# Factors of two levels made behind chosen products, and one sum moved behind a product, in a lightning attention and tanh-shrink kernel

## The chip, the cores and the metric

The kernel runs on one core of a Trainium2 chip. The metric is the device time in microseconds (us) of one execution; lower is better. Before the change it is 693.81 us, the median of three runs (693.71 to 694.52).

## The reference

A causal linear attention with decay runs in blocks, and its output goes through a feed-forward block that keeps `h - tanh(h)`. All is fp32.

```python
# q, k, v: (4, 8, 768, 64); lam: one decay for each of 8 heads
for b in range(nb):                     # blocks of 64 positions, state carried along
    intra = einsum('bhic,bhjc->bhij', qb, kb) * Dmask   # lam ** (i - j) where i >= j
    intra = einsum('bhij,bhjd->bhid', intra, vb)
    inter = einsum('bhid,bhde->bhie', qb * lam_pow, kv_state)
    out[:, :, sl] = intra + inter
    kv_state = lam_block * kv_state + einsum('bhsd,bhse->bhde', kb * rev_pow, vb)
x = out as (4 * 768 tokens, 512)
h = x @ w_in                            # w_in: 512 x 2048
return (h - tanh(h)) @ w_out            # w_out: 2048 x 512
```

## The kernel before, in words

The sequence is cut into six groups of 128 positions; a group is 128 positions of all four batches, 512 tokens. For each group the attention makes its block of x, the "up" product makes h and the activation, and the "down" product makes the output. Group 0 multiplies plainly (`up_plain`, L579, and `down_plain`, L595). While it does, the factors of later groups are made from the weights and stored in a DRAM tensor `factors`. In groups 1 to 5 the two large products use a scheme of seven products for a 2 x 2 split (Winograd's form of Strassen's): for each of them, sums of the four quarters on VectorE (DVE), and seven multiplications on TensorE (PE) instead of eight.

**Up.** The hidden size is cut into four units u. In each unit the products are numbered 1, 2, 6, 5, 7, 4, 3; `up(g, u, n)` makes product n with 8 matmuls records (L393) into one of the PSUM banks y (ya or yb, alternating by unit), z or w. ScalarE (ACT) copies out y (L406, L411, L413) and makes the tanh (L401); DVE adds the banks (L408, L414, L419), takes off the tanh (L402) and makes sums (L422, L423). L414 reads z behind product 5, and product 3 then adds into the same z. Product 1 of the next unit is written ahead of products 4 and 3.

**Down.** The down product also has seven products P1 to P7. P1, P2 and P6 are plain (`down`, L496) and each read four pieces of a factor. P4, P5, P7 and P3 are split once more into seven by the same scheme (`down_twice`, L539), so each needs seven factors of a second level, `fine`. These are made once, in the second group (g = 1), from four quarters of a factor: `load_quarters(n)` brings them from `factors` (L444, issued by GpSimd (POOL)), `factors_twice(n)` makes four sums on DVE (L459) and writes seven tiles to the DRAM tensor `fine` (L461). This happens for four products, TWICE = (4, 5, 7, 3); below they are sets 0 to 3. In the program before, set u is loaded at the start of unit u and made behind product 7 of unit u. P1 is written behind product 7 of the last unit, ahead of that unit's products 4 and 3.

The quarters share a ring of seven SBUF tiles with the pieces of the down products: `piece` (L470 from `fine`, L473 from `factors`) issues loads up to seven ahead of use, on POOL's queue.

**Sums of the hidden block.** Behind P2, `down` makes S2 into tile g11 and then S4 into tile g21 (L508), one instruction per unit for each. Inside `down_twice`, sums s1 and s2 are made by `sums_twice` (L522 to L524), and L544 takes s2 off a quarter once the second of the seven parts was multiplied; the sixth part multiplies that quarter.

**Attention of the next group.** Its pieces are written in between: `run(p0...)` and `run(p1...)`. From group 2 on, q and k come as blocks of 32 x 32 in tiles q_blk and k_blk (L136, 16 DMAs for a tile, issued by SyncE (SP)), in a ring of seven tiles, and DVE transposes them (L271) to qt and kt and scales qt (L281). Loads of all four batches of a group are issued by SP one tile after the other.

The order of each engine's queue is set by the tile framework's scheduler: it takes the program's order as priority and places instructions by its own model of time, so an instruction can stand in its engine's queue ahead of one that is written before it.

Of the kernel before, what the change touches and what calls it, by code (L numbers as in the profile page):

```python
# [14 lines left out]
AL = mybir.AluOpType  # L15
# [8 lines left out]
def kernel(  # L24
# [31 lines left out]
    nc = tc.nc  # L56
# [8 lines left out]
    NU = DFF // 512  # L65
# [312 lines left out]
    def hidden(g, c):  # L378

        if (g, c) not in hid:  # L380
            hid[g, c] = gpool.tile([128, NU, 2, HB], F32, name=f"g{c}", tag=f"g{c}")
        return hid[g, c]

    def up(g, u, n):
        a, bname = FACT[n]
        wt = {"A11": w1[u][:, 0:2, 0], "A12": w1[u][:, 2:4, 0], "S3": w1[u][:, 0:2, 1], "A22": w1[u][:, 2:4, 1],
              "S1": ws[u][:, 0], "S2": ws[u][:, 1], "S4": ws[u][:, 2]}[a]
        x = xt[g][bname] if bname != "B11" else xt[g, 0][:, 0:2]
        key = ("up", g, u)
        t, first = product_bank(key, n)  # L390
        for m in range(2):
            for kt in range(2):
                nc.tensor.matmul(out=t[:, m, :], lhsT=wt[:, kt, ts(m, 128)], rhs=x[:, kt, :],  # L393
                                 start=first and m == 0 and kt == 0, stop=kt == 1, skip_group_check=True)

        def dst(c):
            return hidden(g, c)[:, u]

        def finish(c, src):
            th = work.tile([128, 2, HB], F32, name="th", tag="th")  # L400
            nc.scalar.activation(th, src, AF.Tanh)  # L401
            nc.vector.tensor_tensor(dst(c), src, th, op=AL.subtract)  # L402

        y, z, w = (banks[key, x].rearrange("q (m c) -> q m c", m=2) if (key, x) in banks else None for x in "yzw")
        if n == 1:
            nc.scalar.activation(dst(11), y, AF.Copy)  # L406
        elif n == 2:
            nc.vector.tensor_tensor(dst(11), dst(11), w, op=AL.add)  # L408
            finish(11, dst(11))
        elif n == 6:  # L410
            nc.scalar.activation(dst(12), y, AF.Copy)  # L411
        elif n == 7:
            nc.scalar.activation(dst(22), y, AF.Copy)  # L413
            nc.vector.tensor_tensor(dst(22), dst(22), z, op=AL.add)  # L414
            finish(22, dst(22))
        elif n == 4:
            finish(21, y)
        elif n == 3:
            nc.vector.tensor_tensor(dst(12), dst(12), z, op=AL.add)  # L419
            finish(12, dst(12))  # L420

            nc.vector.tensor_tensor(dst("S1"), dst(12), dst(22), op=AL.add)  # L422
            nc.vector.tensor_tensor(dst(12), dst(11), dst(12), op=AL.subtract)  # L423
# [4 lines left out]
    TWICE = (4, 5, 7, 3)  # L428
# [19 lines left out]
    def load_quarters(n):  # L448
        for i in range(2):
            for j in range(2):  # L450
                quarters[n, i, j] = late["pool"].tile([128, NU, 128], F32, name="wq", tag="wb", bufs=RING)
                factor_block(quarters[n, i, j], XAT[FACT[n][1]], i, j)

    def factors_twice(n):

        b11, b12, b21, b22 = (quarters.pop((n, i, j)) for i in range(2) for j in range(2))
        t1, t2, t4 = (late["pool"].tile([128, NU, 128], F32, name=f"wt{x}", tag="sums", bufs=4) for x in (1, 2, 4))
        for dst, x, y in ((t1, b12, b11), (t2, b22, t1), (b12, b22, b12), (t4, b21, t2)):
            tc.keep_in_program_order(nc.vector.tensor_tensor(dst, x, y, op=AL.subtract))  # L459
        for i, t in enumerate((b11, b21, t2, t1, b12, b22, t4)):  # L460
            nc.gpsimd.dma_start(out=fine[TWICE.index(n), i], in_=t)  # L461
# [23 lines left out]

    res, low = {}, {}

    def down(g, n):

        t, first = product_bank(("down", g), n)  # L490
        a = hidden(g, HIDAT[FACT[n][0]])
        for u in range(NU):
            wb = piece(g, n, u)
            for m in range(2):
                for kt in range(2):
                    nc.tensor.matmul(out=t[:, m, :], lhsT=a[:, u, kt, ts(m, 128)], rhs=wb[:, kt, :],  # L496
                                     start=first and u == 0 and m == 0 and kt == 0, stop=u == NU - 1 and kt == 1,
                                     skip_group_check=True)
        t = t.rearrange("q m c -> q (m c)")
        if n == 1:  # L500
            res[g, 11] = late["pool"].tile([128, 512], F32, name="o11", tag="o11", bufs=1)
            nc.scalar.activation(res[g, 11], t, AF.Copy)
        elif n == 2:
            nc.vector.tensor_tensor(res[g, 11], res[g, 11], t, op=AL.add)
            store(g, 11, res[g, 11])
            for x, y, z in ((11, "S1", 11), (21, 21, 11)):
                for u in range(NU):
                    nc.vector.tensor_tensor(hidden(g, x)[:, u], hidden(g, y)[:, u], hidden(g, z)[:, u], op=AL.subtract)  # L508
        else:
            res[g, "U2"] = otile("u2")  # L510
            nc.scalar.activation(res[g, "U2"], t, AF.Copy)
            nc.vector.tensor_tensor(res[g, 4], res[g, 4], res[g, "U2"], op=AL.add)
# [14 lines left out]
    def down_twice(g, n, zw):  # L527
        a11, a12, a21, a22 = quarter(g, n)
        s1, s2 = low.pop((g, n))
        y = bank("y2", "yb", 1)[:, 0:128]  # L530
        zw = bank("zw", zw, 1)
        o = res[g, n] = otile(f"q{n}")
        r5 = late["pool"].tile([128, 128], F32, name="r5", tag="r5", bufs=2)
        for x, a, dst, keep in ((1, a11, y, o[:, 0:128]), (2, a12, zw[:, 0:128], None), (6, s2, y, o[:, 128:256]),
                                (5, s1, zw[:, 128:256], r5), (7, a21, y, o[:, 384:512]), (3, a12, zw[:, 128:256], None),
                                (4, a22, y, o[:, 256:384])):
            wb = piece(g, n, x).rearrange("p m c -> p (m c)")
            for u in range(NU):
                nc.tensor.matmul(out=dst, lhsT=a[:, u, :], rhs=wb[:, ts(u, 128)], start=x in (1, 2) and u == 0,  # L539
                                 stop=u == NU - 1, skip_group_check=True)  # L540
            if keep is not None:
                nc.scalar.activation(keep, dst, AF.Copy)  # L542
            if x == 2:
                nc.vector.tensor_tensor(a12, a12, s2, op=AL.subtract)  # L544
        nc.vector.tensor_tensor(o[:, 384:512], o[:, 384:512], r5, op=AL.add)
        nc.vector.tensor_tensor(o[:, 0:256], o[:, 0:256], zw[:, 0:256], op=AL.add)
        if n == 5:

            nc.vector.tensor_tensor(res[g, 5], res[g, 5], res[g, "U2"], op=AL.add)
        elif n == 7:  # L550
            nc.vector.tensor_tensor(res[g, 4], res[g, 4], o, op=AL.add)
            store(g, 21, res[g, 4])
            nc.vector.tensor_tensor(o, o, res[g, 5], op=AL.add)
            store(g, 22, o)
        elif n == 3:
            nc.vector.tensor_tensor(o, o, res[g, 5], op=AL.add)
            store(g, 12, o)
# [45 lines left out]
    def run(pieces):  # L603
        for fn, *args in pieces:
            fn(*args)
# [30 lines left out]
            sums_in(kt - KH + NU)  # L636
    early.close()
    late["pool"] = ctx.enter_context(tc.tile_pool(name="late", bufs=1))
    up(1, 0, 1)
    for g in range(1, NG):  # L640
        last = g == NG - 1
        p0, p1 = attention(g + 1) if not last else ([], [])
        for u in range(NU):
            if g == 1:
                load_quarters(TWICE[u])
            for n in (2, 6, 5, 7):
                up(g, u, n)
            if g == 1:
                factors_twice(TWICE[u])
            if u + 1 < NU:  # L650
                up(g, u + 1, 1)
            else:
                down(g, 1)
            up(g, u, 4)
            up(g, u, 3)
            if not last and u > 1:
                run(p0[u - 2:u - 1])
        sums_twice(g, 4)
        down(g, 2)
        run(p0[2:])  # L660
        sums_twice(g, 5)
        down_twice(g, 4, "z")
        run(p1[0:1])
        sums_twice(g, 7)
        down(g, 6)
        run(p1[1:2])
        down_twice(g, 5, "w")
        if not last:
            sums_twice(g, 3)
        run(p1[2:])  # L670
        down_twice(g, 7, "z")
        if not last:
            up(g + 1, 0, 1)
            down_twice(g, 3, "z")
        else:
            down_end(g)
# [30 lines left out]
```

## Time and profile before

| | |
|---|---|
| median of 3 runs | 693.81 us (693.71 to 694.52) |
| profiled execution: time, span | 692.45 us, 690.6 us |
| PE, PEld busy | 671.1, 576.1 us |
| DVE, ACT, POOL busy | 428.3, 191.0, 170.0 us |
| granted clock, mean | 0.995 |
| DMA | 116.43 MB, mean 169 GB/s |
| chain that ended last | PE 84%, issue 6%, DMA 5%, POOL 3% |

The span is the time from the first instruction to the last; the execution's own time has 1.85 us around it. PE is busy for 97% of the span, so the chain of work that ended last is nearly PE's own sequence. PEld is the weight load, which overlaps the matmuls. The slices of the page give the busy share along the span; the second group's up products run from 154 to 200 us, and its down products follow.

### The profile page before, as it was taken

The page shows a single profiled execution, that of the slowest core. Times are in us where ns is not written, and L with a number is a line of the kernel's source. Part 1 is how long each engine was busy: PE and PEld are TensorE (multiplying, and loading weights), DVE is VectorE, ACT ScalarE, POOL GpSimd, SP SyncE. Part 2 cuts the span into 40 slices and gives each one's busy share as a digit, 9 for nine tenths or more (in the row PEclk, how much of TensorE's full clock was granted, in tenths as well). Part 3 has the DMA queues.
Part 4 walks back from the last instruction along what each step waited for, and adds up shares of the span by engine and source line. Part 5 has one row for each costly group of instructions (what it writes and reads, how often), then busy time and mean ns, then how long its engine had stood idle before and what let it go on. Part 6 is the DMA issues. An engine that isn't in the chain of part 4 may idle for free.

```text
span 690.6 us, 12075 instructions
## 1 busy us (share of the span) xinstructions
PE 671.1 (97%) x4568; PEld 576.1 (83%) x4568; DVE 428.3 (62%) x747; ACT 191.0 (28%) x372; POOL 170.0 (25%) x302
## 2 busy tenths in 40 slices
PE   6999999999969999999999999999999999999998
PEld 5788855558758899888899888899988899988897
DVE  3897766995566864347865447766356756354732
ACT  2764433323221112332112332112233112233110
POOL 0001212124643335001244100134200234300252
PEclk9999999999998999999999999999999999999999
DMA  9869959468996688355498902588800366500374
GB/s 189 225 212 235 280 166 257 151 151 251 270 266 201 184 248 237 87 102 111 121 252 238 214 11 46 139 224 229 234 1 10 114 189 199 178 1 1 115 248 155
DMA packets 158393, 116.43 MB, mean 169 GB/s; under 512 B 133120, under 2 KB 133504, under 8 KB 158336
## 3 DMA queue, kind: packets, MB, share of 16 engines
q0 software_dynamic: 25472, 84.95, 37.9%
q1 hardware_dynamic: 132720, 30.71, 23.0%
q8 instruction: 36, 0.59, 0.4%
q14 instruction: 21, 0.17, 0.1%
q10 hardware_dynamic: 144, 0.00, 0.0%
HBM read 94.64 MB, written 20.97 MB: 167 GB/s over the span
## 4 chain that ended last, share of the span: by engine, by line
PE 84%; issue 6%; DMA 5%; POOL 3%; DVE 1%; ACT 1%; POOLq 0%
PE y L393 16%; PE y L496 10%; PE y L539 10%; PE z L393 8%; PE h L579 8%; PE zw L539 7%; PE w L496 5%; PE op L595 4%; PE w L393 4%; PE sp L291 3%; DMA wq<-factors 3%; PE op L342 3%; POOL fine L461 1%; PE kv L311 1%; PE op L336 1%
## 5 line engine op out<-in xcount | busy, mean ns | idle before, releaser
L470 POOL DMA_DIRECT2D wb<-fine x133 | 71.5, 538 | 135.6 <-PE w L496 44.3
L473 POOL DMA_DIRECT2D wb<-factors x64 | 34.7, 544 | 208.5 <-PE y L496 180.3
L496 PE MATMUL y<-wb,g 128*128 128x256 f32 x320 | 73.4, 390 | 6.3 <-issue 6.3
L496 PEld LDWEIGHTS y<-wb,g 128*128 128x128 f32 x320 | 62.3, 196 | 15.3 <-issue 6.7
L393 PE MATMUL y<-xt,w 128*128 128x256 f32 x320 | 73.2, 380 | 0.0
L393 PEld LDWEIGHTS y<-xt,w 128*128 128x128 f32 x320 | 60.5, 190 | 8.5 <-issue 0.5
L401 ACT ACTIVATE th<-g 128x512 f32<-128x512 f32 x60 | 37.7, 630 | 91.6 <-DVE g L419 43.4
L402 DVE TENSOR_TENSOR g<-g,th 128x512 f32<-128x512 f32 x60 | 41.4, 690 | 27.4 <-ACT th L401 27.1
L595 PE MATMUL op<-wt,g 128*128 128x512 f32 x128 | 56.5, 596 | 0.0
L579 PE MATMUL h<-xt,w 128*128 128x256 f32 x256 | 56.1, 381 | 0.0
L579 PEld LDWEIGHTS h<-xt,w 128*128 128x128 f32 x256 | 48.4, 190 | 7.2 <-issue 0.3
L542 ACT ACTIVATE q<-y 128x128 f32<-128x128 f32 x76 | 21.1, 277 | 99.3 <-PE y L539 99.3
L595 PEld LDWEIGHTS op<-wt,g 128*128 128x128 f32 x128 | 23.9, 190 | 27.7 <-issue 27.0
L539 PE MATMUL y<-wb,g 128*128 128x128 f32 x336 | 45.3, 278 | 0.0
L414 DVE TENSOR_TENSOR g<-g,z 128x512 f32<-128x512 f32 x20 | 13.7, 686 | 48.0 <-ACT g L413 48.0
L539 PEld LDWEIGHTS y<-wb,g 128*128 128x128 f32 x336 | 41.2, 192 | 1.1 <-issue 0.3
L393 PE MATMUL z<-tt,ws 128*128 128x256 f32 x160 | 37.9, 380 | 1.1 <-DVE g L419 1.1
L393 PE MATMUL w<-xt,w 128*128 128x256 f32 x160 | 37.8, 379 | 0.0
L393 PE MATMUL y<-tt,w 128*128 128x256 f32 x160 | 37.8, 379 | 0.0
L393 PE MATMUL y<-tt,ws 128*128 128x256 f32 x160 | 37.8, 379 | 0.0
L393 PE MATMUL z<-xt,ws 128*128 128x256 f32 x160 | 37.8, 379 | 0.0
L496 PE MATMUL w<-wb,g 128*128 128x256 f32 x160 | 35.8, 382 | 0.0
(120 smaller groups left out, 1153.3 us busy)
## 6 DMA issues: line engine op xcount, KB each, us to landing
wb<-fine POOLq DMA_DIRECT2D x133, 256.0 KB, 3.6
wb<-factors POOLq DMA_DIRECT2D x64, 256.0 KB, 5.3
raw<-in_moe_w_out_dram POOLq DMA_DIRECT2D x16, 512.0 KB, 4.7
v_nat<-in_v_dram SPq DMA_DIRECT2D x24, 256.0 KB, 5.1
factors<-wt POOLq DMA_DIRECT2D x8, 768.0 KB, 5.3
k_nat<-in_k_dram SPq DMA_DIRECT2D x20, 256.0 KB, 5.1
raw<-in_moe_w_in_dram SPq DMA_DIRECT2D x8, 512.0 KB, 5.0
raw<-in_moe_w_in_dram SPq DMA_DIRECT2D x16, 256.0 KB, 5.6
```

Source lines behind the costliest of these rows:

```text
L291: nc.tensor.matmul(out=sp[j][:, p, :], lhsT=kt[ts(j, 64), p, :], rhs=qt[ts(j, 64), p, :], start=True, stop=True)
L342: nc.tensor.matmul(out=dst(n, p, j), lhsT=vn[:, 2 * p + j, :], rhs=ss[:, j, p, :], start=g == 0 and n == 0 and p % 2 == 0, stop=n == 1 and ...
L393: nc.tensor.matmul(out=t[:, m, :], lhsT=wt[:, kt, ts(m, 128)], rhs=x[:, kt, :], start=first and m == 0 and kt == 0, stop=kt == 1, skip_gro ...
L401: nc.scalar.activation(th, src, AF.Tanh)
L402: nc.vector.tensor_tensor(dst(c), src, th, op=AL.subtract)
L470: nc.gpsimd.dma_start(out=t.rearrange("p m c -> p (m c)"), in_=fine[TWICE.index(n_), SUB.index(x_)].rearrange("p u c -> p (u c)"))
L473: nc.gpsimd.dma_start(out=t, in_=factors[XAT[FACT[n_][1]]][:, 2 * x_:2 * x_ + 2, :])
L496: nc.tensor.matmul(out=t[:, m, :], lhsT=a[:, u, kt, ts(m, 128)], rhs=wb[:, kt, :], start=first and u == 0 and m == 0 and kt == 0, stop=u = ...
L539: nc.tensor.matmul(out=dst, lhsT=a[:, u, :], rhs=wb[:, ts(u, 128)], start=x in (1, 2) and u == 0, stop=u == NU - 1, skip_group_check=True)
L542: nc.scalar.activation(keep, dst, AF.Copy)
L579: nc.tensor.matmul(out=hm[:, m, :], lhsT=w1[u][:, i, a, ts(m, 128)], rhs=xt[0, t][:, i, :], start=m == 0 and i == 0, stop=i == KI - 1, ski ...
L595: nc.tensor.matmul(out=obank[b], lhsT=g, rhs=wt[:, 2 * a:2 * a + 2, :], start=kt == 0 and a == 0, stop=kt == KH - 1 and a == 1)
```

## The change

The quarters of set 0 are loaded ahead of the second group. In that group a counter runs over the products in the order of writing (seven for each unit: 2, 6, 5, 7, then product 1 of the next unit, or P1 behind the last unit, then 4, 3). Behind the 4th, 10th, 15th and 20th of them the sums of set 0, 1, 2 and 3 are written, and at once the loads of the set after it. The 10th is product 5 of unit 1, the 15th is product 2 of unit 2 and the 20th is product 4 of unit 2. So set 3 is written ahead of P1, and not inside unit 3. This only concerns g = 1; the products' own order is the same in all groups.

S4 (into g21) is written behind P4 (`down_twice(g, 4, "z")`) and no longer behind P2; this concerns all five groups. P3, which reads it, comes later still.

```diff
+    def sums_once(g, dst, x, y):
+
+        for u in range(NU):
+            nc.vector.tensor_tensor(hidden(g, dst)[:, u], hidden(g, x)[:, u], hidden(g, y)[:, u], op=AL.subtract)
+
     def down(g, n):
...
             store(g, 11, res[g, 11])
-            for x, y, z in ((11, "S1", 11), (21, 21, 11)):
-                for u in range(NU):
-                    nc.vector.tensor_tensor(hidden(g, x)[:, u], hidden(g, y)[:, u], hidden(g, z)[:, u], op=AL.subtract)
+            sums_once(g, 11, "S1", 11)
...
+    turns, made = (4, 10, 15, 20), []
+    load_quarters(TWICE[0])
     up(1, 0, 1)
     for g in range(1, NG):
...
         for u in range(NU):
-            if g == 1:
-                load_quarters(TWICE[u])
-            for n in (2, 6, 5, 7):
-                up(g, u, n)
-            if g == 1:
-                factors_twice(TWICE[u])
-            if u + 1 < NU:
-                up(g, u + 1, 1)
-            else:
-                down(g, 1)
-            up(g, u, 4)
-            up(g, u, 3)
+            for n in (2, 6, 5, 7, 1, 4, 3):
+                if n != 1:
+                    up(g, u, n)
+                elif u + 1 < NU:
+                    up(g, u + 1, 1)
+                else:
+                    down(g, 1)
+                if g == 1:
+                    made.append(n)
+                    if len(made) in turns:
+                        t = turns.index(len(made))
+                        factors_twice(TWICE[t])
+                        if t + 1 < len(TWICE):
+                            load_quarters(TWICE[t + 1])
             if not last and u > 1:
                 run(p0[u - 2:u - 1])
         sums_twice(g, 4)
...
         down_twice(g, 4, "z")
+        sums_once(g, 21, 21, 11)
         run(p1[0:1])
```

The lines of the kernel after the change stand a few further down: L496 becomes L501, L508 becomes L491, L539 becomes L542 and L544 becomes L547; L459 and what is ahead of it stay.

## The prediction

> **What bounds the kernel now.** I read the page's busy shares first: TensorE (PE) is busy 671.1 of 690.6 us, so only its gaps can be won and any new gap is lost in full. The waits of PE say where the gaps are; the two that lie in the second group (the stretch from 154 to 240 us) are:
>
> ```profile
> PE y L496 <- issue: 6.3, 1, 6.3
> PE z L393 <- DVE g L419: 1.1, 1, 1.1
> ```
>
> The first is the start of product P1 (down, n = 1), at 206.84 us; the profile names no releaser. The windows view shows what the pause costs beyond itself. Its columns are the length, then the busy time of PE, PEld, DVE, ACT and POOL, the granted clock, the share of the DMA engines, and GB/s:
>
> ```profile
> 204.00:206.00 2.00, 0.00 (x0) 0.00 (x0) 1.55 (x3) 0.42 (x1) 0.55 (x1) 0.83 0.92 265
> 207.00:208.00 1.00, 1.00 (x3) 0.82 (x4) 0.00 (x0) 0.00 (x0) 0.00 (x0) 0.50 0.49 142
> 212.00:213.00 1.00, 1.00 (x6) 0.81 (x5) 0.52 (x1) 0.00 (x0) 0.00 (x0) 0.92 0.88 175
> ```
>
> The clock halves at 205.33 (0.83 over 2 us is two thirds at 1.00 and a third at 0.50) and is whole again at 212.16 (0.92 likewise). PE works at half rate from 206.84 to 212.16, 5.32 us, and loses 2.66. The chain shows P1 taking 9.78 us where later P1s take 6.91. So this place costs 6.30 + 2.87, and with the 1.1 us wait 10.3 us in all: the most that the change can win.
>
> The DVE timeline (start, duration, what, idle before and its releaser) shows the work that is moved, and the place that decides my forecast:
>
> ```profile
> 175.57 0.69 DVE L414 TENSOR_TENSOR g<-g,z 128x512 f32<-128x512 f32 x1 [2.42 <-ACT g L413]
> ...
> 181.51 0.69 DVE L459 TENSOR_TENSOR wt<-wq,wt 128x512 f32<-128x512 f32 x1 [3.26 <-DMA wq<-factors]
> 182.12 0.69 DVE L459 TENSOR_TENSOR wq<-wq 128x512 f32<-128x512 f32 x1
> ...
> 235.94 0.69 DVE L544 TENSOR_TENSOR g<-g,s 128x512 f32<-128x512 f32 x1 [1.28 <-PE zw L539]
> ...
> 239.89 0.71 DVE L271 STREAM_TRANSPOSE qt<-q_blk 128x512 f32<-128x512 f32 x1
> 240.52 0.67 DVE L271 STREAM_TRANSPOSE kt<-k_blk 128x512 f32<-128x512 f32 x1
> 241.12 0.65 DVE L281 TENSOR_TENSOR qd<-qt,fwd 128x512 f32<-128x512 f32 x1
> 241.69 0.70 DVE L271 STREAM_TRANSPOSE qt<-q_blk 128x512 f32<-128x512 f32 x1
> 245.55 0.71 DVE L271 STREAM_TRANSPOSE kt<-k_blk 128x512 f32<-128x512 f32 x1 [3.16 <-DMA q_blk<-in_q_dram]
> ```
>
> L544 subtracts s2 inside down_twice(1, 4), the TensorE product P4, and PE's sixth part of P4 needs its result:
>
> ```profile
> 238.42 1.06 PE L539 MATMUL zw<-wb,g 128*128 128x128 f32 x8
> ```
>
> The last transpose, kt of the fourth batch (b = 3), waits until 245.55 for its tile. The SP timeline says why it is so late:
>
> ```profile
> 210.44 9.85 SPq L136 DMA_DIRECT2D k_blk<-in_k_dram  x16
> 220.81 11.96 SPq L136 DMA_DIRECT2D q_blk<-in_q_dram  x16
> 232.88 7.54 SPq L136 DMA_DIRECT2D k_blk<-in_k_dram  x16
> ```
>
> The eight tiles of group 2 (16 issues each) leave SP one after the other from 156.53; k_blk of b = 3 is the eighth and leaves at 232.88 to 240.42.
>
> [...] L459 waits 3.26 us for its quarter and the next instruction, L402 at 183.32, waits behind it. [...] 16 SP issues take 7.5 us while the engines are 23% busy (287.82 on) and 11.96 at 79%.
>
> **The change, part by part.** Nothing is added or taken out; the compiled order has the same matmuls in the same order on PE. What moves:
>
> (a) *Factors on DVE.* There are four sets of four quarters; each takes four subtractions L459, about 0.605 us apart. Set 0 keeps its place. Set 1 now stands ahead of L414 of unit 1 (it was behind). It still needs its fourth quarter, which POOL issues at 176.60 behind set 0's stores, all unchanged, so the wait still ends at 181.51. L414, done by 176.26 before, then starts at 181.51 + 3 x 0.605 = 183.32 and ends at 184.0. PE's n = 3 of unit 1 adds into the bank z that L414 reads: 178.19 becomes 184.05, a new wait of **5.9 us** in place of the 1.1. [...] Set 2 stands ahead of L414 of unit 2; with PE 6 us later it is done first, no cost. Queued behind the waiting L459: L414, L402, L419, L408, and ScalarE's tanh for them, all paid in that 5.9.
>
> (b) *Factors on POOL.* The order of loads and stores changes little: the same 19 transfers lie between 181.9 us and the last quarter's load, and they land about 1 us apart (the share of the DMA engines is 0.84 from 150 to 200), so that load lands near 204.4 as before, and the first piece of P1 still arrives near 206. PE now gets there at about 205 to 207.5, so the 6.3 us wait is mostly gone.
>
> (c) *Set 3* now stands ahead of P1 on DVE, and behind it four instructions and six of the next attention (L271, L281), then L402 of unit 3, which P1's last quarter needs: 204.4 + 7 x 0.605 + 3.7 + 0.7 = 213.0, so P1 ends at 214.8, against 216.6. **The factor part is worth about -1.7 us (-1 to -2.2)**: most of the gap is moved forward, not removed. The fourth piece of P1 no longer waits for a ring slot that P1 frees.
>
> (d) *S4* (four subtractions L508, g21) is written behind P4. Its own cost is nothing: 4 x 0.61 us of DVE in the cover of P2 and of P4. But the scheduler fills the place differently. In the compiled order of every group the second half's transposes (L271 qt, kt, L281, L271 qt, L316, L271 kt, L281) now stand **ahead of L544**. In the second group the last kt waits for k_blk of b = 3. SP's order is the same up to there, so it leaves SP near 240.4 (239 to 242; the traffic of these 40 us is the same, in another order), and lands 1.7 to 5.4 us later (medians of the blocks between 286 and 304 and between 228 and 242 are 1.7 and 3.5; the last before took about 5). PE will have stopped, and with it the refills of the ring, so I take 242.7. Then 0.63 + 0.57 + 0.69 for kt, L281, L544 and 0.1 of signals: PE's sixth part of P4 starts at 244.7 instead of 238.42, **+6.3 us**. PE comes there at about 236.8, having won 1.7, and idles 7.9 us, so the clock halves: +2.6 (I take the 2.66 of before[...]). Because this wait ends with SP's transfer, it swallows what (a) to (c) win or lose.
>
> (e) *Groups 3 to 5.* The same reordering, but the tiles are there: SP sends the eighth of group 3 at 315.01 to 322.7, and L544 comes near 343. The 3.9 us of transposes fit ahead of it (P4 starts at 341.4, its sixth part at 345.9). SP's two moved loads (k_nat, v_nat) are used tens of us later. Cost 0.
>
> Sum: +6.3 + 2.6 = **+8.9 us**. The profiled execution took 692.45 us (span 690.60 and 1.85 around it) and would become 701.3; the median of the three runs is 693.81, 1.36 above it, so I forecast **702.7**.
>
> **Rivals.**
> 1. *The tile is there in time.* If k_blk of b = 3 landed before about 235, L544 would not wait, and the factor part would decide: 693.81 - 1.7 = 692.1, faster. It needs SP to send its last 64 blocks in about 33 us where it took 41.5. For: 7.5 us for 16 is possible with quiet engines. Against: these 40 us carry the fine factors and the ring.
> 2. *The wait is short*, 1 to 3 us[...] and cancels the 1.7: 693 to 695, no difference. It needs a landing near 237.
> 3. *The intended effect*: both gaps go, 693.81 - 10.3 = 683.5. Against: the fourth quarter of set 1 cannot land before 181.4, and DVE keeps its order.
> 4. *The transfer is as late as before* (245.4) or later[...].
>
> **How the numbers follow.** Main case, [...] 0.87, rival 4 within it. Rival 1: 0.06. Rival 2: 0.05. Rival 3: 0.02. A measurement of this kernel tells about 0.2%, 1.4 us, from no change. Slower 0.88 (main and a little of rival 2), same 0.05, faster 0.07. The range 698.0 to 707.5 is the main case with its ends; what is left out, below it, is 0.13 and the main case's own tails.
>
> **What would show it.** Right: the waits of PE list a DVE L544 (line 547 after) for zw of 6 to 10 us near 237 to 245, with the clock at 0.50 behind it; the DVE timeline shows L271 waiting for a DMA just ahead of it; a wait of z for L414 of 5 to 6 us near 178 to 184; P1's wait of 6.3 gone or under 2. Wrong: no PE gap between 230 and 250; then rival 1 or 3. If L414's wait is missing, step (a) is wrong; if P1 still waits 6 us, (b) is.

## The result, and the profile after

| | before | after |
|---|---|---|
| median | 694.05 us (693.71 to 694.52, 4 runs) | 701.94 us (701.07 to 702.6, 4 runs) |
| profiled execution: time, span | 692.45, 690.6 us | 701.07, 699.0 us |
| PE, DVE busy | 671.1, 428.3 us | 672.3, 426.5 us |
| granted clock, mean | 0.995 | 0.99 |

The changed kernel is slower: the ratio is 1.0112, with an interval of 1.0095 to 1.013, or 7.9 us between the medians. The work is the same; PE's busy time grows by 1.2 us only. What grows is PE's idle time, so the waits of PE are read first (columns: us in total, times, longest):

```profile
PE zw L542 <- issue: 7.7, 1, 7.7
PE z L393 <- DVE g L414: 6.0, 1, 6.0
...
PE zw L542 <- ACT q L545: 1.7, 2, 0.9
```

Before, there were 6.3 us at P1 (y L496) and 1.1 us at z L393 behind L419. P1's wait is not in the list any more. In its place stands one wait in the up product and one inside P4; the last line, two short waits in later groups, is taken up under (e). PE's timeline (start, duration, what, idle before) puts them in time:

```profile
185.41 3.78 PE L393 MATMUL z<-xt,ws 128*128 128x256 f32 x8 [6.05 <-DVE g L414]
...
209.01 7.28 PE L501 MATMUL y<-wb,g 128*128 128x256 f32 x32
...
245.03 2.05 PE L542 MATMUL zw<-wb,g 128*128 128x128 f32 x8 [7.67 <-issue]
...
248.58 7.33 PE L501 MATMUL y<-wb,g 128*128 128x256 f32 x32
```

P1 at 209.01 has no bracket: it starts without a pause. The pause of 7.67 us is at the sixth part of P4. "issue" says that the profile names no releaser; DVE's timeline shows which instruction it was, and what that one waited for:

```profile
182.86 0.69 DVE L459 TENSOR_TENSOR wt<-wq,wt 128x512 f32<-128x512 f32 x1 [7.84 <-DMA wq<-factors]
...
184.67 0.68 DVE L414 TENSOR_TENSOR g<-g,z 128x512 f32<-128x512 f32 x1
...
235.67 0.65 DVE L316 TENSOR_TENSOR state<-state,kv 128x512 f32<-128x512 f32 x1
243.05 0.71 DVE L271 STREAM_TRANSPOSE kt<-k_blk 128x512 f32<-128x512 f32 x1 [6.72 <-DMA q_blk<-in_q_dram]
243.68 0.65 DVE L281 TENSOR_TENSOR qd<-qt,fwd 128x512 f32<-128x512 f32 x1
244.25 0.68 DVE L547 TENSOR_TENSOR g<-g,s 128x512 f32<-128x512 f32 x1
```

The subtraction L547, on which the sixth part depends, ends at 244.93, and PE starts at 245.03. L547 itself waited for nothing; it stood behind a transpose that waited for its tile. (The bracket names a q_blk transfer; the tile that the transpose reads is k_blk, and with the factors alone, below, the same wait is named by k_blk.) SP issued that tile in this stretch:

```profile
231.19 7.64 SPq L136 DMA_DIRECT2D k_blk<-in_k_dram  x16
```

The windows (length; busy time of PE, PEld, DVE, ACT, POOL; clock; DMA share; GB/s) give two stretches in which the clock was at half rate:

```profile
184.00:186.00 2.00, 0.59 (x2) 0.51 (x3) 1.35 (x3) 0.61 (x2) 1.00 (x2) 0.56 1.08 242
190.00:192.00 2.00, 2.00 (x9) 1.65 (x8) 0.75 (x2) 0.63 (x1) 0.46 (x1) 0.73 0.96 271
241.00:243.00 2.00, 0.00 (x0) 0.00 (x0) 0.00 (x0) 0.00 (x0) 0.00 (x0) 0.82 0.40 78
248.00:250.00 2.00, 2.00 (x10) 1.81 (x10) 0.00 (x0) 0.28 (x1) 0.54 (x1) 0.73 0.67 159
```

Both begin while PE stands still (0.62 over 184 to 185, 0.64 over 242 to 243) and last on behind its start. Their ends are an estimate that takes the clock to be 0.50 or 1.00 (it reads 0.50 over 188 to 190 and over 243 to 245, and 1.00 over 182 to 183 and over 252 to 254): 0.73 over 2 us is 1.08 us at half rate, so the first ends at 191.08, and likewise the second at 249.08.

Step by step, after less before in the two profiled executions: the second group's first product starts 1.0 us late (155.03 against 154.02). That is ahead of the moved work. The same start lies at 153.40 in a kernel below with the same early load and at 155.85 in one without it, so it is spread between executions. Product 3 of unit 1 is 7.2 us late (185.41 against 178.19). Product 4 behind P1 is 0.3 us early (216.13 against 216.45). The sixth part of P4 is 6.6 us late (245.03 against 238.42), P6 behind it 8.4 (248.58 against 240.20), and the end of the span 8.4.

### The profile page after: what moved, and what is told of

Read it like the earlier page. It is cut to its first block, busy times and chain, and to the rows that moved or that the text cites. A ratio compares the mean times of both kernels' runs of the same rounds, so it can differ in the third digit from the quotient of the medians.

```text
span 699.0 us, 12071 instructions
## 1 busy us (share of the span) xinstructions
PE 672.3 (96%) x4568; PEld 577.4 (83%) x4568; DVE 426.5 (61%) x747; ACT 191.1 (27%) x372; POOL 170.0 (24%) x302
## 4 chain that ended last, share of the span: by engine, by line
PE 86%; issue 6%; DMA 4%; POOL 2%; DVE 1%; ACT 1%; SPq 0%; POOLq 0%
PE y L393 18%; PE y L542 10%; PE y L501 10%; PE z L393 9%; PE h L582 8%; PE zw L542 8%; PE w L501 5%; PE w L393 5%; PE op L598 4%; PE sp L291 3%; PE op L342 3%; DMA wq<-factors 2%; PE op L336 1%; DMA raw<-in_moe_w_in_dram 1%; PE kv L311 1%
## 5 line engine op out<-in xcount | busy, mean ns | idle before, releaser
L393 PE MATMUL y<-xt,w 128*128 128x256 f32 x320 | 73.2, 379 | 0.0
L501 PE MATMUL y<-wb,g 128*128 128x256 f32 x320 | 71.2, 380 | 0.0
L501 PEld LDWEIGHTS y<-wb,g 128*128 128x128 f32 x320 | 60.6, 191 | 8.4 <-DVE g L402 0.3
L393 PEld LDWEIGHTS y<-xt,w 128*128 128x128 f32 x320 | 60.5, 190 | 8.5 <-issue 0.5
L542 PE MATMUL y<-wb,g 128*128 128x128 f32 x336 | 46.1, 281 | 0.0
L393 PE MATMUL z<-xt,ws 128*128 128x256 f32 x160 | 39.7, 393 | 6.0 <-DVE g L414 6.0
L542 PEld LDWEIGHTS y<-wb,g 128*128 128x128 f32 x336 | 42.1, 195 | 1.1 <-issue 0.3
L414 DVE TENSOR_TENSOR g<-g,z 128x512 f32<-128x512 f32 x20 | 13.7, 686 | 45.1 <-ACT g L413 45.1
L393 PEld LDWEIGHTS z<-xt,ws 128*128 128x128 f32 x160 | 31.4, 197 | 10.9 <-DVE g L414 6.4
L542 PE MATMUL zw<-wb,g 128*128 128x128 f32 x224 | 30.9, 281 | 9.4 <-issue 7.7
L393 PE MATMUL w<-xt,w 128*128 128x256 f32 x160 | 38.8, 387 | 0.0
L393 PE MATMUL y<-tt,ws 128*128 128x256 f32 x160 | 37.8, 379 | 0.0
L393 PE MATMUL z<-tt,ws 128*128 128x256 f32 x160 | 37.8, 379 | 0.0
```

## The experiments

The theory: the late k tile, reached through the new order on DVE, costs the time, and it comes with the move of S4 alone. The rivals were that both parts are needed for the loss, that the new order itself costs and not the late tile, and that the factor part hurts.

**S4 behind P4 alone.** The kernel before, with one edit; the factors stay as they were.

```diff
-            for x, y, z in ((11, "S1", 11), (21, 21, 11)):
-                for u in range(NU):
-                    nc.vector.tensor_tensor(hidden(g, x)[:, u], ...)
+            sums_once(g, 11, "S1", 11)
...
         down_twice(g, 4, "z")
+        sums_once(g, 21, 21, 11)
         run(p1[0:1])
```

> Only S4 is written behind P4; the factors are made as before. Theory A (the loss is the second half's transposes standing ahead of L544, where the last one waits for the k block of batch 3): the old gap of 6.3 us at P1 is back, but PE then meets the same wait for that block, which ends with SP's transfer near 242 to 244, so the time is that of the whole change within 2 us: 700 to 703.5. Rival B (the loss is the new 6 us wait of bank z for L414, made by the factor part): without the factor part the time is that of before, 693 to 695.

It took 702.01 us (701.0 to 707.58, 6 runs) beside 693.55 for the kernel before: 1.0132 (1.0106 to 1.0158). The waits of PE, then lines of the timelines of DVE and PE, then windows of this kernel:

```profile
PE zw L542 <- issue: 8.0, 1, 8.0
PE y L501 <- DMA fine<-wq: 6.2, 1, 6.2
```

```profile
245.90 0.71 DVE L271 STREAM_TRANSPOSE kt<-k_blk 128x512 f32<-128x512 f32 x1 [7.05 <-DMA q_blk<-in_q_dram]
...
247.88 2.05 PE L542 MATMUL zw<-wb,g 128*128 128x128 f32 x8 [8.00 <-issue]
```

```profile
242.00:244.00 2.00, 0.00 (x0) 0.00 (x0) 0.00 (x0) 0.00 (x0) 0.00 (x0) 0.51 0.76 209
252.00:254.00 2.00, 2.00 (x10) 1.72 (x9) 0.00 (x0) 0.00 (x0) 0.48 (x1) 0.93 0.51 139
```

The time is in the expected range. The move of S4 makes the whole loss alone, with the same pause in the same place, while P1 still pauses for 6.2 us. The loss does not need the factors' part.

**Factors alone.** The changed kernel with S4 put back behind P2.

```diff
             sums_once(g, 11, "S1", 11)
+            sums_once(g, 21, 21, 11)
...
         down_twice(g, 4, "z")
-        sums_once(g, 21, 21, 11)
```

> Only the factors are moved; S4 stays behind P2. Theory A: the transposes stand behind L544 again, nothing swallows the factor part, and it is worth 1 to 2.4 us: 691.5 to 693, with the z wait of 6 us still there and P1's wait gone. Rival B: the z wait makes it slower than before, 698 to 702.

It took 691.20 us (690.55 to 692.2, 6 runs): 0.9962 (0.9948 to 0.9976), or 2.6 us less (1.7 to 3.6). That is just below the 691.5 to 693 expected. Its waits of PE, PE's timeline at P1 and at the last of these waits, and the transpose of the k tile:

```profile
PE z L393 <- DVE g L414: 6.1, 1, 6.1
...
PE kv L311 <- PE op L342: 1.8, 3, 0.6
PE y L501 <- DMA wb<-factors: 1.0, 1, 1.0
```

```profile
207.34 7.07 PE L501 MATMUL y<-wb,g 128*128 128x256 f32 x32
...
661.15 5.45 PE L501 MATMUL y<-wb,g 128*128 128x256 f32 x24 [1.02 <-DMA wb<-factors]
```

```profile
243.58 0.71 DVE L271 STREAM_TRANSPOSE kt<-k_blk 128x512 f32<-128x512 f32 x1 [3.39 <-DMA k_blk<-in_k_dram]
```

The tile is as late here as in the changed kernel (243.58 against 243.05), but nothing that PE needs stands behind the transpose: the subtraction of s2 began at 233.74. P1, at 207.34, starts without a pause; its 6.3 us come back as 6.1 us at product 3 of unit 1. The wait of 1.0 us on L501 is another one, in P6 of the last group.

**The k tile of batch 3 not loaded.** The changed kernel, where group 2 takes the k tile of batch 2 again in place of that of batch 3. It leaves out this load of 16 DMAs; the order on PE, DVE and POOL is that of the changed kernel.

```diff
-            load_blocks(g, 3, "k")
+            if g == GB:
+                raw[g, 3]["kb"] = raw[g, 2]["kb"]
+            else:
+                load_blocks(g, 3, "k")
```

> The whole change, with the k block of batch 3 in group 2 not loaded (batch 2's is transposed in its place; this part of the computation is left out). The order on PE, DVE, ACT and POOL is that of the change, only the transfer that is waited for is gone. Theory A: no wait at the sixth part of P4, 691.5 to 693.5. Rival C (the reordering itself costs, or the wait is for something else): stays near 702.

It took 691.70 us (690.77 to 693.28, 9 runs): 0.9979 (0.9965 to 0.9993). The time is in the expected range. The transpose, the subtraction of s2 and the sixth part, from the timelines of DVE and PE, and the same waits in the list (lines are 3 further down here):

```profile
235.69 0.69 DVE L274 STREAM_TRANSPOSE kt<-k_blk 128x512 f32<-128x512 f32 x1
...
236.88 0.68 DVE L550 TENSOR_TENSOR g<-g,s 128x512 f32<-128x512 f32 x1
...
237.66 1.13 PE L545 MATMUL zw<-wb,g 128*128 128x128 f32 x8 [0.85 <-ACT q L548]
```

```profile
PE zw L545 <- ACT q L548: 2.6, 3, 0.9
```

The order stayed, the late tile went, and with it nearly all of the pause. What is left of it, 0.85 us, is the order's own price: the subtraction L550, behind the transposes, ends 0.1 us before the sixth part starts (the bracket names a copy of ACT). The list shows this wait three times, once in each of three groups. The order alone thus costs little; the order together with the late tile makes the loss.

**S4 behind the attention piece.** The changed kernel with two lines exchanged, so that the transposes' place is fixed before S4 is written.

```diff
         down_twice(g, 4, "z")
-        sums_once(g, 21, 21, 11)
         run(p1[0:1])
+        sums_once(g, 21, 21, 11)
```

> The whole change with two written lines exchanged: S4 behind the first piece of the second attention half and not ahead of it. The transposes are pinned behind the DVE instruction written last before them, which is P4's L546 again instead of S4's last subtraction; S4 itself stays where it was in the DVE queue. Theory A: 691.5 to 693, as with the factors alone. Rival B: near 700; rival C: near 702.

It took 689.86 us (688.05 to 691.73, 6 runs): 0.9941 (0.9923 to 0.9959), faster than both kernels and below the 691.5 to 693 expected. DVE's timeline around P4, and PE's longest wait in this group:

```profile
235.38 0.69 DVE L547 TENSOR_TENSOR g<-g,s 128x512 f32<-128x512 f32 x1 [0.59 <-PE zw L542]
...
244.25 0.71 DVE L271 STREAM_TRANSPOSE kt<-k_blk 128x512 f32<-128x512 f32 x1 [2.43 <-DMA q_blk<-in_q_dram]
```

```profile
PE z L393 <- DVE g L414: 5.3, 1, 5.3
```

L547 is back ahead of the transposes, and PE does not feel the late tile. It is S4's line in the program that turned the order. The code suggests how: the transposes are written with `keep_in_program_order`, which, read from the code and the compiled orders, ties an instruction behind the one written last before it on the same engine. Before, that one was the last addition of P4 (L546), behind L544. After, it is S4's last subtraction, which is ready behind P2 and is placed early; the transposes then may go ahead of L547 too. That this tie is the cause agrees with this run and with the compiled orders; the tie itself was not tried apart.

S4's late place also has a gain that was not looked for. With the factors alone, and before, the attention's state product (kv L311) waits 0.6 us in three groups; here none of these waits is listed. In the second group kv starts there at 230.48, 0.1 us behind the end of DVE's L306 (229.69, 0.69 us), which stands behind the four sums of S4; here L306 begins at 227.30, ahead of these sums. The 1.8 us agree with most of what this kernel is faster than the one with the factors alone (689.86 against 691.20), but were not tried apart.

What is left here is the wait of z, and 0.94 and 0.66 us in P1. The next three runs ask whether the wait of z is a loss of its own or P1's old gap in another place.

**Set 1 behind product 7.** As the last kernel, with set 1's sums one product later, behind L414 in DVE's queue.

```diff
-    turns, made = (4, 10, 15, 20), []
+    turns, made = (4, 11, 15, 20), []
```

> As the run before it (S4 behind the attention piece), with set 1 behind the 11th product, product 7 of unit 1, where it was before the change, and no longer behind the 10th. Theory A (the gap of the second group is set by the transfers of the fine factors and P1's pieces, and the factor part only moves it): the 6 us wait of z goes back to about 1 us, PE comes to P1 about 5 us earlier and waits there for its first piece by about as much, so the time stays within 1.5 us of that run: 688.5 to 692. Rival D (the wait of z is a pure loss that DVE's order makes): 6 to 8 us are won, 682 to 684.

It took 689.21 us (686.33 to 690.15, 5 runs): 0.9941 (0.9922 to 0.9961), the same as without the edit. The profiled execution is the fastest of the five, so its waits may be somewhat shorter than usual. DVE and PE:

```profile
192.33 0.69 DVE L459 TENSOR_TENSOR wt<-wq,wt 128x512 f32<-128x512 f32 x1 [4.31 <-DMA wq<-factors]
...
194.88 3.24 PE L393 MATMUL z<-xt,ws 128*128 128x256 f32 x8 [3.53 <-DVE g L414]
```

The wait is gone from unit 1 and stands at unit 2, where set 2's sums are ahead of that unit's L414. The time is as the theory expected and not 6 to 8 us less, the place is not: it expected it at P1. As the wait only moved to another z, the run does not show what that wait costs by itself.

**Set 3 behind P1.** As the kernel with the lines exchanged, but sets 1 and 2 are made behind product 7 of their units, and set 3 is loaded behind P1 and made behind product 3 of the last unit.

```diff
-    turns, made = (4, 10, 15, 20), []
+    turns, made = (4, 11, 18), []
...
+                    if len(made) == 26:
+                        load_quarters(TWICE[3])
+                    if len(made) == 28:
+                        factors_twice(TWICE[3])
...
-                        if t + 1 < len(TWICE):
+                        if t + 1 < 3:
...
```

> As e5, with sets 1 and 2 behind product 7 of their units and set 3 loaded only behind P1 and made behind product 3 of the last unit, so that P1's pieces go ahead of it in POOL's queue. Theory A: P1's pieces land by 200 and both gaps of the second group go, but for 1 us at z: about 8 to 9 us less than before, 684 to 686, if set 3's four ring slots and stores do not hold up P4's pieces; if they do, a wait of 2 to 5 us stands in P4 and the time is 686 to 690. Rival D: no better than e5.

It took 688.79 us (686.07 to 689.13, 6 runs): 0.9922 (0.9902 to 0.9942). That is in the second of the two expected ranges. P1 starts without a wait and the up products lose 0.8 us only, but P4 pauses twice. POOL and PE:

```profile
201.35 7.07 PE L501 MATMUL y<-wb,g 128*128 128x256 f32 x32
...
220.94 0.75 POOL L444 DMA_DIRECT2D wq<-factors  x1 [2.38 <-DVE wt L459]
...
228.35 1.13 PE L542 MATMUL y<-wb,s 128*128 128x128 f32 x8 [1.54 <-DVE s L526]
...
232.91 2.08 PE L542 MATMUL zw<-wb,s 128*128 128x128 f32 x8 [3.43 <-DMA wb<-fine]
```

The last quarter of set 3 leaves only at 220.94 (the view names the first sum of the set as what it waited for), so the sums that need it are late on DVE ahead of L526, and the pieces of P4 that are queued on POOL behind the set's stores come late too. Of the 6.3 us at P1 in the kernel before, 5.0 now stand in P4. In time this kernel and the one before it are not apart, so rival D is not excluded.

**Set 3 late, S4 as before.** The kernel before with only that move of set 3.

```diff
-            if g == 1:
+            if g == 1 and u + 1 < NU:
                 load_quarters(TWICE[u])
...
-            if g == 1:
+            if g == 1 and u + 1 < NU:
                 factors_twice(TWICE[u])
...
+            if g == 1 and u + 1 == NU:
+                load_quarters(TWICE[u])
             up(g, u, 4)
             up(g, u, 3)
+            if g == 1 and u + 1 == NU:
+                factors_twice(TWICE[u])
```

> The kernel before with one edit: set 3 loaded behind P1 and made behind product 3 of the last unit; sets 0 to 2 and S4 as before. Theory A: P1's pieces no longer queue behind set 3, the 6.3 us gap goes, and the time is as that of e6 within 1.5 us (S4's place is worth nothing by itself): 684 to 688. Rival E (S4's late place is a gain of its own of over 1 us): e6 is faster than this by that.

It took 689.03 us (688.48 to 689.78, 4 runs): 0.9937 (0.9918 to 0.9956), a little over the 684 to 688 expected. P1 has no pause; the longest in the group is now in the attention. The list of waits, then DVE and PE:

```profile
PE kv L311 <- issue: 2.7, 1, 2.7
```

```profile
224.09 0.69 DVE L459 TENSOR_TENSOR wt<-wq,wt 128x512 f32<-128x512 f32 x1 [1.97 <-issue]
...
226.50 0.68 DVE L306 TENSOR_TENSOR k_nat<-k_nat,mask 128x512 f32<-128x512 f32 x1
...
227.28 0.69 PE L311 MATMUL kv<-v_nat,k_nat 128*64 128x64 f32 x16 [2.70 <-issue]
```

The product kv starts 0.1 us behind the end of L306, and L306 stands behind set 3's sums, of which the second (L459) waited until 224.09. So this pause, too, comes from set 3.

Without any of the other moves this one is worth 4.4 us (3.1 to 5.7). The kernel with set 3 behind P1 is 0.24 us faster between the medians, so rival E's gain of over 1 us is not seen. The last three kernels lie within 0.5 us of each other; which of them is best stays open.

## Why the prediction was right

The forecast was 702.7 us, slower, and the median is 701.94. Of its rivals, that of a tile there in time describes the kernel without the k load: it said 692.1, and that kernel took 691.70. Where terms that were off cancelled, it is said below. One sign came under another name: the list of waits names no DVE L547 but "issue", and DVE's timeline shows that it was L547.

- **(a), the wait at product 3 of unit 1:** right. It forecast 5.9 us; 6.05 came, behind L414, which stood behind L459. PE started 1.4 us later than the forecast 184.05, as the quarter came that much later, and about 1.0 of this is the group's later start. The clock's share, for which the forecast had no figure, was 2.8: half rate from PE's start at 185.41 to 191.08, halved.
- **(b), P1's wait:** right, and the kernel with the factors alone shows it apart: nothing is left of the 6.3 us. PE's arrival was forecast too early: it came to P1 at 209.01, 208.0 without the group's later start, where 205 to 207.5 was said. The clock's 2.8 of (a) was not carried over in full.
- **(c), the factor part:** the right sign, and the size perhaps too small. It forecast -1.7 (-1 to -2.2); the kernel with this part alone came to -2.6 (-1.7 to -3.6), an interval that begins at the forecast. In the profiled executions it looks like the forecast up to P4: the sixth part starts at 236.22 against 238.42, of which 0.6 is that run's earlier start of the group (153.40 against 154.02), so -1.6. Its span is only 1.2 us shorter (689.4 against 690.6), as P6 of the last group then waits 1.0. What else the medians hold isn't settled.
- **(d), the turned order and the late tile:** right, and shown from three sides: alone it makes the loss, without the late tile there is none, and with the order put back there is none. That the moment was met is in part luck: two terms were off and nearly cancelled. The tile left SP at 238.83, where 240.4 was taken; it could be read 4.2 us later (243.05), where 2.3 was taken because PE's pause would quiet the transfers. The engines' share did fall to 0.40 (241 to 243, above), and the tile was not quicker. The transpose then began 0.35 us after the forecast 242.7. The clock's share, forecast at 2.6 from P1's pause of 6.3 us before, was less: from 245.03 to 249.08 at half rate, halved, is 2.0, and between the sixth part (6.6 late) and P6 (8.4 late) there are 1.8.
- **(e), groups 3 to 5:** right in the sum, but not for the reason given. The delay is 8.6 us at the attention behind P6 (255.84 against 247.21) and 8.4 at the end, so the later groups add nothing. Yet the transposes do not quite fit ahead of L547: the sixth part of P4 waits 0.85 us in the third and in the fourth group (354.63 and 462.28), as in the kernel without the k load. At the same time the waits of 0.6 us of kv L311, which stand in these groups before, are gone, because S4's sums no longer stand ahead of L306. The forecast had neither term, and they nearly cancel.
- **The sum** said +8.9 against the profiled execution; it was +8.6 there (701.07 less 692.45): 6.6 for the wait, where 6.3 was said, and 2.0 of clock, where 2.6 was. How much of the 6.6 is the group's later start is open: SP's row began 1.0 us late too (157.53 against 156.53), but its last tile left 1.6 us earlier than before. The forecast then added the 1.36 us by which the median lay above the profiled execution; after the change this is 0.87. The two differences make up nearly all of the 0.76 us between 702.7 and 701.94. The ends of the forecast's range, 698.0 and 707.5, were the author's estimate.
- **"It swallows what (a) to (c) win":** S4 alone came to 1.0132 (1.0106 to 1.0158), and with the factors' part as well to 1.0112 (1.0095 to 1.013). The intervals overlap: a gain of the factors' part is not seen while the tile decides.

## What to carry to other kernels

When an instruction that is ready early is moved to a new place in the program, look at what is tied to the place and not only at the instruction: here four subtractions that cost nothing of their own let transposes pass the subtraction that PE waits for. Ahead of a reorder, ask of each instruction that moves forward in an engine's queue when its transfer lands and what will stand behind it: here L547, which waited for nothing itself, stood behind a transpose that waited 6.72 us, and a wait of 3 us that nobody stood behind became 7.7 us of PE. And a pause fed by one long row of transfers moves when the sums are moved (6.3 us at P1 became 6.1 at product 3 with the factors alone); to shorten it, take a set out of the row until later (4.4 us with set 3 alone), and check what the later transfers then delay.

## What the runs showed of the hardware

Behind its two long pauses in the changed kernel PE worked at a granted clock of 0.50 (over 188 to 190 and over 246 to 248) and took about twice as long: the eight matmuls of product 3 took 3.78 us in unit 1, behind the pause (185.41), and 1.89 us in unit 2 (200.38). What a pause cost in this way did not go by its length alone. The losses below are estimates from the windows and timelines. In the kernel with the lines exchanged:

```profile
184.00:186.00 2.00, 0.72 (x2) 0.64 (x3) 1.30 (x4) 0.74 (x2) 1.04 (x2) 0.84 0.94 233
186.00:188.00 2.00, 2.00 (x7) 1.55 (x6) 1.30 (x2) 0.86 (x2) 2.00 (x5) 0.50 0.99 342
188.00:190.00 2.00, 2.00 (x9) 1.69 (x8) 0.69 (x1) 0.23 (x1) 2.00 (x4) 0.81 1.04 337
```

Against 1.00 these windows lose 0.32, 1.00 and 0.38 us, 1.7 in all. A pause of 5.3 us here and one of 6.05 in the changed kernel, 0.8 us apart, thus cost 1.7 and 2.8 us of clock. Shorter pauses cost as much. With set 1 behind product 7, PE paused 3.53 us, and behind it the clock read 0.62 over 195 to 197 and 0.53 over 197 to 199, which lose 0.76 and 0.94 us, again 1.7. With set 3 behind P1, it paused 1.54 us and, one part of P4 later, 3.43 us, and the last four parts of P4 then took 6.45 us (232.91 to 239.36), where the same four take 3.57 with set 1 behind product 7 (232.77 to 236.34): that is 2.9 more. And the longest pauses did not cost the most: 7.67 us in the changed kernel cost 2.0, and 8.00 us with S4 alone cost 2.2 (half rate from 247.88 to 252.28, by the 0.93 over 252 to 254). What sets the loss beside the length was not shown.
